# A planner-ordered attention and MLP kernel: the order planned with other durations, and batch 0's stores on another queue

## The chip, the cores and the metric

The kernel runs on one core of one Trainium2 chip. The metric is the time of the device in microseconds (us) from start to end of one execution.

## What is computed

A linear attention with positional weights is followed by a two-layer MLP with squared ReLU. Shapes: q, k, v are 8 batches x 8 heads x 576 positions x 64; the MLP maps 4608 tokens of width 512 to 2048 and back.

```python
theta = np.pi / 2.0 * pos / S            # pos = 0..575, S = 576
phi(x) = concatenate([relu(x) * cos(theta), relu(x) * sin(theta)])
kv  = einsum('bhsf,bhsd->bhfd', phi(k), v)
z   = sum(phi(k), axis=2)
num = einsum('bhsf,bhfd->bhsd', phi(q), kv)
den = einsum('bhsf,bhf->bhs', phi(q), z)[..., None] + 1e-06
x   = (num / den) as (tokens, 512)
out = relu(x @ w_in) ** 2 @ w_out        # float32
```

## The kernel before

**Tiles.** Each batch's 576 positions are four tiles of 128 tokens (J = 4) and a tail of 64. Per batch the work has these stages. A feature operation on ScalarE or VectorE makes relu(x) times the cosine or the sine for q and k (`declare_feature`, lines 406 and 408 in the profile), and a cast makes v bf16 (`declare_v`, line 413). TensorE forms kv and z per head (`declare_kz`; 65 columns, one being the sum), q is transposed, and the numerator and denominator follow (`declare_num`, which also divides on VectorE, lines 637 to 639). For batches 0 and 1 the transposing of q and x is done on TensorE (lines 591, 682), for batches 2 to 7 by DMA on the SyncE queue (`qpT`, `xT`, lines 575 and 667).

**The MLP.** Batches 0 to 2 multiply x by w1 plainly (`declare_plain`); batches 3 to 7 use seven products in place of eight (`declare_seven1`, with sums of x blocks from `declare_x_sums`). ReLU is on ScalarE (line 416), the square on VectorE (line 419), and VectorE's combined add and ReLU is line 422. The second layer is plain for batch 0 (`declare_rows`) and seven products for pairs of tiles after that (`declare_pair`, with sums of g blocks, `gs`, and of w2, `w2s`). All matmuls but the transposing ones are recorded at line 430, all VectorE sums at line 427. Tails of several batches go through the MLP together.

**Queues.** q, k and v of batch 0 are loaded from SyncE (SP) in a fixed prologue, w1 in four quarters from GpSimd (POOL). Loads of batches 1 and 2 and of w2 are on POOL, later ones on SP. Output is stored from a tile `ysb` (line 391): batch 0's two stores from POOL, the others from SP. The queue is chosen by `st_name` and `st_eng`.

**What sets the order.** The functions above only declare operations: an engine or a choice of engines with a duration in microseconds, the keys read and written, and for TensorE a place `pos`. A `Planner` then goes through a simulated time: at each step it takes the operation that can start earliest, by these durations, by free buffers and by a transfer's time, and among equals the one with the smallest slot (TensorE) or latest allowed time (`late`). The result is the order in which each engine gets its instructions. At run time each engine executes its list in order and waits on semaphores; the simulated times themselves have no effect. `SHIFTS` is a list of corrections: `81:-5.0` adds -5.0 us to the slot or `late` of operation number 81 in the order of declaration, and a third field (`:ACT`, `:DVE`) fixes its engine. The fourth argument of the planner is a margin added to the landing of every planned transfer:

```python
T_MM, T_MM128, T_MM65, T_TR = 0.1092, 0.0586, 0.0296, 0.066
plan = Planner(POOLS, 4.5, ("gs1", "gs2", "gs3", "gs4"), 1.0, SHIFTS)
...
o.done = pipe + (self.margin if e != "GIVEN" else 0.0)
```

In `declare_att(b, kpos, npos, cos_k, cos_q, cast)` the last three arguments are the engines allowed for the cosine features of k, those of q, and the casts of v; the defaults are either engine, VectorE and ScalarE.

Of the kernel before, what the change touches and what calls it, by code (L numbers as in the profile page):

```python
# [18 lines left out]


SHIFTS = """
23:9.5:ACT 37:-0.5 38:1.0 44:17.5:ACT 46:-1.0 53:-0.5 62:11.5 79:-2.0 85:-2.5 89:3.0 93:11.0
108:5.5 144:9.0 152:-2.0 157:9.5:ACT 191:-5.0 194:-1.0 202:-1.5 203:-3.5:ACT 204:2.0 210:3.0
238:2.5 241:2.5 243:5.0 249:-6.0 257:-4.0 260:-2.0 261:-6.0 270:2.5 271:3.5 287:-5.0 325:-2.0
335:-0.5 340:1.5 348:8.5 354:-7.0 364:-19.0 383:1.0 390:-3.5 392:1.0 417:-4.5 487:-5.0 492:1.5
516:-7.5 517:-5.5 530:39.0 533:25.5 546:9.0 563:5.5 565:12.5 573:-8.5 575:5.0 588:13.0 593:4.5
598:-2.0 611:-4.5 617:-5.5 636:-1.5 670:7.5 677:-2.0 690:1.0 698:0.0:DVE 702:22.5 703:-19.5
704:3.5:ACT 706:-4.0 715:2.0 731:-2.5 748:5.0 781:-4.5 783:-6.0 785:-7.0 787:-2.0 790:-1.0
794:-1.5 797:1.0 799:1.0 807:11.0 813:-5.5 817:-4.0 820:-7.0 822:-5.5 836:-3.5 850:-3.5
859:-34.0 860:-15.0 870:1.0 872:-4.0 884:12.0 890:49.0 893:17.0 906:5.5 907:23.5 911:3.0 917:3.0  # L30
936:-3.0 951:-12.5 957:-1.0 958:-1.5 963:-3.5 985:7.0 990:-4.0 998:3.5 1005:-4.5 1009:5.5
1023:-10.0 1024:-8.5 1030:-10.0 1041:-26.0:ACT 1042:-10.5 1133:-13.0 1143:1.5 1155:4.0 1157:3.0
1176:-4.5 1191:4.5 1209:5.5 1247:2.5 1306:-0.5
"""


# [197 lines left out]
def kernel(  # L234
# [9 lines left out]
    nc = tc.nc  # L244
# [7 lines left out]
    J = S // P  # L252
    MAIN = J * P
    TAIL = S - MAIN
    HH = H // 2
# [64 lines left out]
    def bank(buf):  # L320
        return banks[:, buf.i + (6 if buf.pool == "B" else 0), :]
# [104 lines left out]
    def sub(out, in0, in1, op=ALU.subtract):  # L426
        nc.vector.tensor_tensor(out=out, in0=in0, in1=in1, op=op)  # L427
# [102 lines left out]
    def declare_kz(b, pos, engs=("ACT",)):  # L530
        ba, bb = plan.buf("F"), plan.buf("F")
        kvz = kvzb[b] = plan.buf("kvz")
        for j in range(NS):

            def kz(_, j=j):
                kp, vx = at(kp_of(b, j)), at(vxb[b, j])
                for hh in range(HH):
                    for half in range(2):
                        h = half * HH + hh
                        if j < J:  # L540
                            lhsT, rhs = kp[:, h, :], vx[:, h, :]
                        else:
                            p0, p1 = half * TAIL, (half + 1) * TAIL
                            lhsT, rhs = kp[p0:p1, hh, :], vx[p0:p1, hh, :]
                        mm(
                            bank_pair(ba, bb)[:, half, hh * E1 : (hh + 1) * E1],
                            lhsT,
                            rhs,
                            j == 0 and hh == 0,
                            j == J and hh == HH - 1,  # L550
                        )

            add(
                ("PE", T_MM65 * (2 if j < J else 1) * HH + 0.02),
                kz,
                r=[(kp_of(b, j), j % 2, "c"), (kp_of(b, j), j % 2, "s"), vxb[b, j]],
                w=[ba, bb],
                pos=pos + 0.001 * j,
            )

        def kvz_copy(eng):
            dst = at(kvz).rearrange("p (a h) e -> p a (h e)", a=2)
            copy(eng, dst, bank_pair(ba, bb)[:, :, 0 : HH * E1])

        add({e: 0.5 if e == "ACT" else 0.6 for e in engs}, kvz_copy, r=[ba, bb], w=[kvz])
# [39 lines left out]
    def declare_num(b, j, pos):  # L605
        n = 2 if j < J else 1
        bks = [plan.buf("F") for _ in range(n)]
        pe = (b, "p", j) in qpTb
        qT = qpTb[b, "p", j] if pe else qpTb[b, j // 2]
        den = plan.buf("den")  # L610
        xbuf = x_of(b, j)

        def num(_):
            kvz, t = at(kvzb[b]), at(qT)
            h0 = 0 if pe or j == J else j % 2 * H
            for hh in range(HH):
                for half in range(2):
                    e0 = hh * E1
                    if j < J:
                        o = bank_pair(*bks)[:, half, e0 : e0 + E1]  # L620
                        lhsT = t[:, h0 + half * HH + hh, :]
                    else:
                        p0, p1 = half * TAIL, (half + 1) * TAIL
                        o = bank(bks[0])[p0:p1, e0 : e0 + E1]
                        lhsT = t[:, hh, p0:p1]
                    mm(o, lhsT, kvz[:, half * HH + hh, :], True, True)

        add(("PE", T_MM65 * n * HH + 0.015), num, r=[qT, kvzb[b]], w=bks, pos=pos)

        def div(_):  # L630
            if n == 2:
                n4 = bank_pair(*bks)
            else:
                n4 = banks[:, bks[0].i : bks[0].i + 1, :]
            n4 = n4[:, :, 0 : HH * E1].rearrange("p b (h e) -> p b h e", e=E1)
            d, r = at(den)[:, 0, 0:n], at(den)[:, 1, 0:n]
            nc.vector.tensor_single_scalar(out=d, in_=n4[:, :, :, D], scalar=EPS, op=ALU.add)  # L637
            nc.vector.reciprocal(out=r, in_=d)
            nc.vector.tensor_tensor(  # L639
                out=x_at(b, j).rearrange("p (b k) (l d) -> p b k l d", b=n, l=2),  # L640
                in0=n4[:, :, :, 0:D].rearrange("p b (k l) d -> p b k l d", l=2),
                in1=r.rearrange("p b (k l) -> p b k l", l=2)
                .unsqueeze(4)
                .to_broadcast([P, n, HH // 2, 2, D]),
                op=ALU.mult,
            )

        add(("DVE", 1.06 if j < J else 0.75), div, r=bks, w=[den, (xbuf, j % 2)])
# [147 lines left out]
    def declare_x_sums(b):  # L796
        buf = xsb[b] = plan.buf("xs")
        x0, x1 = xT_of(b, 0), xT_of(b, 1)
        a = lambda kk, half: at((x0, x1)[half])[:, kk * KB2 : (kk + 1) * KB2, :]
        t = lambda n: a(0, 1) if n == 3 else at(buf)[:, min(n, 3) - 1]  # L800
        xk = [[(x0, 0), (x0, 1)], [(x1, 0), (x1, 1)]]
        for n, ops, reads in (
            (1, lambda: (a(0, 1), a(0, 0)), xk[0] + xk[1]),
            (2, lambda: (a(1, 1), t(1)), xk[1] + [(buf, 1)]),
            (3, lambda: (a(1, 1), a(0, 1)), xk[1]),
            (4, lambda: (a(1, 0), t(2)), xk[0] + [(buf, 2)]),
        ):
            add(("DVE", 0.34), lambda _, n=n, ops=ops: sub(t(n), *ops()), r=reads, w=[(buf, n)] + (xk[1] if n == 3 else []))

    def declare_seven1(b, r, t):  # L810

# [11 lines left out]
        def product(name, off, acc, w, x, first, reads):  # L823
# [24 lines left out]
        product("P4", 13, Bk, lambda: w1_cols(1, 1, r), lambda: Tn(4), False, [key(1), (xs, 4)])  # L848
        add(("ACT", 0.5), lambda _: relu(block(1, 0), halves(bank(Bk))), r=[Bk], w=[(rows[1], 0)])
        add(  # L850
            ("DVE", 0.63), lambda _: add_relu(block(1, 1), halves(bank(E)), halves(at(u3))),
            r=[E, u3], w=[(rows[1], 1)],
        )
        product("P3", 14, E, lambda: w1_sum(4, r), lambda: X(1, 1), False, [("w1s", 4, r)] + xk[1])
        add(
            ("DVE", 0.63), lambda _: add_relu(block(0, 1), halves(bank(E)), halves(at(u2))),
            r=[E, u2], w=[(rows[0], 1)],
        )
        for i in range(2):
            hb = i * HBH + 2 * r  # L860
            if last:
                for j in range(2):
                    add(
                        ("DVE", 0.34),
                        lambda _, i=i, j=j, hb=hb: square(gT[:, hb : hb + 2, j * TP : (j + 1) * TP], block(i, j)),
                        r=[(rows[i], j), turn], w=[gkey(hb, j)],
                    )
            else:
                add(
                    ("DVE", 0.6), lambda _, i=i, hb=hb: square(gT[:, hb : hb + 2, :], at(rows[i])),  # L870
                    r=[(rows[i], 0), (rows[i], 1), turn], w=[gkey(hb, 0), gkey(hb, 1)],
                )
# [1 line left out]


    def st_name(b):
        return "SP" if b >= 1 else "POOL"

    def st_eng(b):
        return nc.sync if b >= 1 else nc.gpsimd  # L880

    def w2_block(i, j):
        return w2sb[:, i * HBH : (i + 1) * HBH, j * DM2 : (j + 1) * DM2]
# [38 lines left out]
    def declare_pair(b, pair, t):  # L922
# [7 lines left out]
        for n, ops, op, reads in (  # L930
# [2 lines left out]
            (3, lambda: (a(0, 0), a(1, 0)), ALU.subtract, gk(0)),  # L933
            (4, lambda: (a(0, 1), at(gs[2])), ALU.subtract, gk(1) + [gs[2]]),
        ):
            add(("DVE", 0.67 if n == 1 else 0.61), lambda _, n=n, ops=ops, op=op: sub(at(gs[n]), *ops(), op), r=reads, w=[gs[n]])
        acc = lambda x: bank(x)[:, 0:DM2]
        yb = lambda i, j: at(y)[:, i, j * DM2 : (j + 1) * DM2]
        u2, u3 = (lambda: at(u)[:, 0:DM2]), (lambda: at(u)[:, DM2:DM])
# [317 lines left out]
    declare_load(1, "v", "POOL", 23.0)  # L1257
    declare_w2_load(2, 25.0, 12.0)
    declare_w2_load(3, 26.0, 13.0)
    declare_att(1, T2[0] + 4.5, [T2[0] + x for x in (6.0, 9.0, 12.0, 14.0, 19.0)], BOTH, BOTH, BOTH)  # L1260
    for nm in "qkv":
        declare_load(2, nm, "POOL", 28.0)
    declare_rows(0, range(4), T2[0], 2)
    for s in range(8):
        for i in range(2):
            declare_plain(1, s % 4 * 4 + 2 * i, s // 4, T1[1] + s * 2 * PROD2 + i * PROD2, s == 0)
    declare_att(2, T2[1], [T2[1] + 1.7 + 1.75 * i for i in range(NS)], BOTH, BOTH, BOTH)
    for nm in "qkv":
        declare_load(3, nm, "SP", after=[turned["q", 2, J // 2]])
    declare_w2_sums()  # L1270
# [71 lines left out]
```

## Time and profile before

| | |
|---|---|
| three runs | 276.74, 278.27, 279.21 us (median 278.27) |
| profiled execution, its own time | 276.82 us |
| its span, first to last instruction | 274.8 us |
| TensorE matmul busy | 267.9 us (98%) |
| TensorE weight loads busy | 227.6 us (83%) |
| VectorE, ScalarE, GpSimd busy | 218.9, 194.9, 21.6 us |
| data moved | 53.01 MB, mean 193 GB/s |

The span is shorter than the execution's own time by 2.0 us. PE is TensorE's matmuls, PEld its weight loads, DVE VectorE, ACT ScalarE, POOL GpSimd, and SP SyncE, whose q stands for the queue's own instructions. A start time counts from the span's start. Matmuls overlap in the pipeline, so a group's length is more than the distance to the next group's start.

### The profile page before, as it was taken

How to read it: one execution, taken by the hardware profiler on the slowest of the kernel's cores; microseconds unless marked ns; L12 is line 12 of the kernel's file. 1: busy time of each engine (PE TensorE's matmuls, PEld its weight loads, DVE VectorE, ACT ScalarE, POOL GpSimd, SP SyncE). 2: the span in 40 equal slices, each digit the busy share in tenths (PEclk: the TensorE clock that was granted, in tenths of full speed). 3: DMA queues.
4: the chain of work that ended last, by engine and by line, in shares of the span. 5: the costliest groups of instructions: out<-in, count | busy, mean ns of one | idle time of the engine just before them, and what ended most of it. 6: DMA issues, size and time to landing. Idle time of an engine off the chain costs nothing.

```text
span 274.8 us, 7115 instructions
## 1 busy us (share of the span) xinstructions
PE 267.9 (98%) x2845; PEld 227.6 (83%) x2845; DVE 218.9 (80%) x515; ACT 194.9 (71%) x391; POOL 21.6 (8%) x38
## 2 busy tenths in 40 slices
PE   8979999999999999999999999999999999999994
PEld 3668856789988988888888898988988888888884
DVE  1789996997694989699968999799968798279652
ACT  3876982997895598589957994699735954684522
POOL 1453544010000000000000000000000000000000
PEclk9999999999999999999999999999999999999999
DMA  7999999969979998899299955996198301200025
GB/s 217 321 205 290 296 283 365 219 218 225 361 160 186 281 334 156 224 347 221 81 164 308 259 181 102 265 338 217 35 205 170 91 2 44 95 16 2 1 79 153
DMA packets 81840, 53.01 MB, mean 193 GB/s; under 512 B 53584, under 2 KB 77648, under 8 KB 81808
## 3 DMA queue, kind: packets, MB, share of 16 engines
q1 hardware_dynamic: 75136, 40.12, 58.4%
q0 software_dynamic: 6528, 12.32, 17.1%
q8 instruction: 22, 0.36, 0.5%
q10 hardware_dynamic: 144, 0.13, 0.1%
q14 instruction: 10, 0.08, 0.1%
HBM read 36.70 MB, written 9.44 MB: 168 GB/s over the span
## 4 chain that ended last, share of the span: by engine, by line
PE 80%; DMA 8%; DVE 7%; issue 1%; SPq 1%; POOL 1%; ACT 1%; DVEq 0%
PE banks L430 79%; DMA w1sb<-in_moe_w_in_dram 4%; DMA qpT<-qp 2%; DMA vt<-in_v_dram 2%; DVE rs L422 2%; DVE gT L419 2%; DVE gs L427 2%; PE banks L591 1%; DVE x L639 1%; POOL w1sb L373 1%; SPq L366 0%; PE banks L682 0%; DVE qp L408 0%; DVE kp L408 0%; SPq L358 0%
## 5 line engine op out<-in xcount | busy, mean ns | idle before, releaser
L430 PEld LDWEIGHTS <-w1sb 128*128 128x128 bf16 x784 | 73.0, 98 | 10.4 <-DMA w1sb<-in_moe_w_in_dram 1.4
L430 PE MATMUL banks<-xT,w1sb 128*128 128x256 bf16 (+1 forms) x576 | 68.4, 267 | 1.0 <-DMA w1sb<-in_moe_w_in_dram 1.0
L430 PEld LDWEIGHTS <-gs 128*128 128x128 bf16 x512 | 49.0, 98 | 5.9 <-DVE gs L427 0.2
L416 ACT ACTIVATE rt<-banks 128x512 bf16<-128x512 f32 x64 | 37.2, 600 | 14.9 <-PE banks L430 9.3
L430 PEld LDWEIGHTS <-gT 128*128 128x128 bf16 x400 | 38.0, 98 | 9.0
L430 PE MATMUL banks<-w2sb,gT 128*128 128x256 bf16 (+1 forms) x288 | 44.2, 296 | 0.0
L430 PEld LDWEIGHTS <-w1s 128*128 128x128 bf16 x320 | 30.7, 98 | 3.7
L430 PE MATMUL banks<-w2sb,gs 128*128 128x256 bf16 x256 | 33.0, 273 | 0.0
L430 PE MATMUL banks<-w2s,gs 128*128 128x256 bf16 x256 | 32.2, 273 | 0.0
L422 DVE CUSTOM_DVE_ANT_0 rs<-banks,sums 128x512 bf16<-128x512 f32 x40 | 27.0, 684 | 4.5 <-ACT sums L847 3.1
L419 DVE TENSOR_TENSOR gT<-rs 128x1024 bf16<-128x1024 bf16 (+1 forms) x50 | 27.7, 579 | 1.8 <-ACT rs L416 1.0
L416 ACT ACTIVATE rs<-banks 128x512 bf16<-128x512 f32 x40 | 23.6, 604 | 3.1 <-PE banks L430 2.9
L430 PE MATMUL banks<-xs,w1s 128*128 128x256 bf16 x160 | 23.0, 273 | 0.0
L430 PE MATMUL banks<-xT,w1s 128*128 128x256 bf16 x160 | 22.9, 273 | 0.0
L419 DVE TENSOR_TENSOR gT<-rt 128x512 bf16<-128x512 bf16 x48 | 19.2, 418 | 4.5 <-ACT rt L416 4.3
L427 DVE TENSOR_TENSOR ysb<-banks,sums 128x256 f32<-128x256 f32 x32 | 13.4, 418 | 11.2 <-PE banks L430 7.3
L406 ACT ACTIVATE qp<-q,sin_col 128x512 bf16<-128x512 f32 x31 | 22.1, 738 | 0.1
L639 DVE TENSOR_TENSOR x<-banks,den 128x512 bf16<-128x512 f32 x30 | 20.7, 691 | 1.0
L406 ACT ACTIVATE kp<-k,sin_col 128x512 bf16<-128x512 f32 x30 | 21.2, 734 | 0.0
L427 DVE TENSOR_TENSOR gs<-gT 128x1024 bf16<-128x1024 bf16 x28 | 19.2, 686 | 1.1 <-PE banks L430 0.7
L413 ACT CAST vx<-v 128x512 bf16<-128x512 f32 x26 | 16.2, 636 | 0.9 <-DMA v<-in_v_dram 0.9
L637 DVE TENSOR_SCALAR den<-banks 128x8 f32<-128x8 f32 (+1 forms) x38 | 6.0, 159 | 12.5 <-PE banks L430 12.3
(106 smaller groups left out, 364.0 us busy)
## 6 DMA issues: line engine op xcount, KB each, us to landing
out_dram<-ysb SPq DMA_DIRECT2D x13, 512.0 KB, 3.5
k<-in_k_dram SPq DMA_DIRECT2D x6, 1024.0 KB, 6.4
v<-in_v_dram SPq DMA_DIRECT2D x5, 1024.0 KB, 7.9
q<-in_q_dram SPq DMA_DIRECT2D x5, 1024.0 KB, 9.3
w1sb<-in_moe_w_in_dram POOLq DMA_DIRECT2D x4, 512.0 KB, 10.5
q<-in_q_dram POOLq DMA_DIRECT2D x2, 1024.0 KB, 11.2
w2sb<-in_moe_w_out_dram POOLq DMA_DIRECT2D x4, 512.0 KB, 11.6
k<-in_k_dram POOLq DMA_DIRECT2D x2, 1024.0 KB, 11.3
```

The lines of the kernel that those rows point to most:

```text
L373: nc.gpsimd.dma_start(out=w1sb[:, :, f0:f1], in_=moe_w_in[:, f0:f1].rearrange("(kb p) f -> p kb f", p=P),)
L406: nc.scalar.activation(out=dst, in_=src, func=ACTF.Relu, scale=col)
L413: (nc.scalar.copy if eng == "ACT" else nc.vector.tensor_copy)(out=out, in_=in_)
L416: nc.scalar.activation(out=out, in_=in_, func=ACTF.Relu)
L419: nc.vector.tensor_tensor(out=out, in0=in_, in1=in_, op=ALU.mult)
L422: nc.vector._custom_dve(TENSOR_ADD_SAT, out=out, in0=in0, in1=in1, s0=float("inf"), s1=0.0)
L427: nc.vector.tensor_tensor(out=out, in0=in0, in1=in1, op=op)
L430: nc.tensor.matmul(out=out, lhsT=lhsT, rhs=rhs, start=start, stop=stop, skip_group_check=True)
L591: nc.tensor.transpose(t[:, h, :], qp_at(b, j)[:, h, :], ident[:, :])
L637: nc.vector.tensor_single_scalar(out=d, in_=n4[:, :, :, D], scalar=EPS, op=ALU.add)
L639: nc.vector.tensor_tensor(out=x_at(b, j).rearrange("p (b k) (l d) -> p b k l d", b=n, l=2), in0=n4[:, :, :, 0:D].rearrange("p b (k l) d -> ...
```

## The change

It has four kinds of edits. The output stores of batch 0 go to the SP queue like all others. Durations given to the planner change: the tail groups of kv and numerator count eight small matmuls where they counted four, and several VectorE sums, squares and adds get 0.01 to 0.09 us more. For batches 1 and 2 the engines that may do the cosine features (and for batch 1 the casts) are restricted to VectorE. And `SHIFTS` is another list. Of the long list a few entries are shown.

```diff
 SHIFTS = """
-... 79:-2.0 85:-2.5 89:3.0 93:11.0 ... 690:1.0 ... 859:-34.0 860:-15.0 ... 1023:-10.0 1024:-8.5 1030:-10.0 ...
+... 81:-5.0 85:-8.5 89:7.0 91:1.0 92:3.5 97:2.5 102:2.0 ... 690:14.0 691:4.5 ...
+... 856:-5.0 857:-6.0 859:-9.0 ... 1024:-34.5 1026:-36.0 1030:-20.0 ...
 """
...
-                ("PE", T_MM65 * (2 if j < J else 1) * HH + 0.02),
+                ("PE", T_MM65 * (2 * HH) + 0.02),
...
-        add(("PE", T_MM65 * n * HH + 0.015), num, r=[qT, kvzb[b]], w=bks, pos=pos)
+        add(("PE", T_MM65 * 2 * HH + 0.015), num, r=[qT, kvzb[b]], w=bks, pos=pos)
...
-            add(("DVE", 0.34), lambda _, n=n, ops=ops: sub(t(n), *ops()), ...
+            add(("DVE", 0.43 if n == 3 else 0.36), lambda _, n=n, ops=ops: sub(t(n), *ops()), ...
...
-            ("DVE", 0.63), lambda _: add_relu(...        # twice in declare_seven1
+            ("DVE", 0.64), lambda _: add_relu(...
...
-                        ("DVE", 0.34),                   # the square of a batch's last round
+                        ("DVE", 0.37),
...
     def st_name(b):
-        return "SP" if b >= 1 else "POOL"
+        return "SP" if b >= 0 else "POOL"
     def st_eng(b):
-        return nc.sync if b >= 1 else nc.gpsimd
+        return nc.sync if b >= 0 else nc.gpsimd
...
-            add(("DVE", 0.67 if n == 1 else 0.61), ... w=[gs[n]])
+            add(("DVE", 0.72 if n == 1 else 0.62), ... w=[gs[n]])
...
-    declare_att(1, T2[0] + 4.5, [...], BOTH, BOTH, BOTH)
+    declare_att(1, T2[0] + 4.5, [...], DVE1, DVE1, DVE1)
...
-    declare_att(2, T2[1], [...], BOTH, BOTH, BOTH)
+    declare_att(2, T2[1], [...], DVE1, DVE1, BOTH)
```

The planner's call, with its margin, is not in the diff.

## The prediction

> **What bounds the kernel now.** I read four views in this order: the busy shares, the matmul timeline, the waits, and the busy time by stage. The first two lines are of the page.
>
> ```profile
> PE 267.9 (98%) x2845; PEld 227.6 (83%) x2845; DVE 218.9 (80%) x515; ACT 194.9 (71%) x391; POOL 21.6 (8%) x38
> ...
> PEclk9999999999999999999999999999999999999999
> ```
>
> TensorE is busy for 267.9 of 274.8 us at the full granted clock. That leaves 6.9 us of idle time, and 1.2 us of it lies ahead of the first matmul and 3.4 us behind the last, which ends at 271.3 us. A busy share hides small stalls, so I looked at distances between starts in the timeline of the matmuls. Its columns are start, length, engine, line, operation and count, and in brackets the idle time before.
>
> ```profile
> 17.72 1.06 PE L430 MATMUL banks<-xT,w1sb 128*128 128x128 bf16 x16
> 19.64 1.05 PE L430 MATMUL banks<-xT,w1sb 128*128 128x256 bf16 x8 [0.86 <-DMA w1sb<-in_moe_w_in_dram]
> 20.52 0.41 PE L430 MATMUL banks<-kvz,sums 128*128 128x65 bf16 x8
> 20.77 1.03 PE L430 MATMUL banks<-xT,w1sb 128*128 128x256 bf16 x8
> 21.64 0.39 PE L682 MATMUL banks<-ident,x 128*128 128x128 bf16 x4
> 22.19 1.05 PE L430 MATMUL banks<-xT,w1sb 128*128 128x256 bf16 x8 [0.16 <-DMA w1sb<-in_moe_w_in_dram]
> ...
> 122.35 1.04 PE L430 MATMUL banks<-xTt,w1sb 128*128 128x256 bf16 x8
> 123.73 0.60 PE L430 MATMUL banks<-xs,w1sb 128*128 128x256 bf16 x4 [0.34 <-ACT sums L847]
> ...
> 142.47 0.60 PE L430 MATMUL banks<-xT,w1sb 128*128 128x256 bf16 x4
> 143.26 0.42 PE L430 MATMUL banks<-kvz,qpT 128*128 128x65 bf16 x8 [0.20 <-DMA qpT<-qp]
> ```
>
> Eight matmuls of 256 columns start 0.87 us before the next group (20.77 to 21.64), so one takes 0.109 us; one of 128 columns takes 0.056 us (23.07 to 23.29 for four), one of 65 takes 0.030 us. From these the stalls follow. 17.72 plus 16 x 0.057 is 18.63, and the next group starts at 19.64: 1.01 us, for the second quarter of w1. 21.64 plus 0.22 is 21.86, then 22.19: 0.33 us, for the third quarter. 122.35 plus 0.87 is 123.22, then 123.73: 0.51 us. 142.47 plus 0.44 is 142.91, then 143.26: 0.35 us. The same sum on the group of 97.97 us gives 0.18 us. Together these five make 2.38 us. Between 13.2 and 16.5 us, where batch 0's attention is a chain through all engines, another 1.0 us is lost. So **3.4 us is all that a better order can win**; the rest is matmul work, start and end.
>
> The tail of each batch (64 tokens) shows a third thing.
>
> ```profile
> 40.53 1.14 PE L430 MATMUL banks<-vx,kp 128*128 128x65 bf16 x32
> 41.59 0.30 PE L430 MATMUL banks<-vxt,kpt 64*128 64x65 bf16 x8
> 41.83 1.04 PE L430 MATMUL banks<-w2sb,gT 128*128 128x512 bf16 x4
> ```
>
> 40.53 plus 32 x 0.0296 is 41.48; the next full-size group begins at 41.83. The eight tail matmuls cost 0.35 us, where the planner counts 4 x 0.0296 + 0.02 = 0.14 us.
>
> **What the Trainium skill says.** "Trainium Kernel Development and Optimization", Performance Expectations, calls matmul busy time a bad metric because matmuls are pipelined; this trace agrees, since 98% busy holds the stalls just worked out. "TensorEngine Tiling (Array Packing)", Key Properties, says that changing the tiling mode drains TensorE; that fits the 0.35 us, about 0.1 us on each side of the eight small matmuls. "DMA: Bandwidth & Descriptors", Issuing engines are not separate DMA queues, says that the SP and POOL queues run on the same engines and that another issuer saves issue time alone. The page of before gives 3.5 us (SP) and 4.9 us (POOL) from issue to landing of a 512 KB store, at different loads.
>
> **Part 1: batch 0's stores from POOL to SP.** Two transfers of 512 KB change their queue.
>
> ```profile
> 52.37 0.61 POOL L391 DMA_DIRECT2D out_dram<-ysb  x1 [6.07 <-ACT ysb L1020]
> 55.54 0.69 POOL L391 DMA_DIRECT2D out_dram<-ysb  x1 [2.55 <-ACT ysb L1020]
> ...
> 51.14 11.44 SPq L575 DMA_TRANSPOSE qpT<-qp  x2
> ```
>
> They are POOL's last two instructions, so its 8.6 us of waiting held up nobody and is worth nothing when it goes. SP gets two issues of about 0.4 us (its stores later show 0.38 and 0.53), into a gap: the line of 51.14 us is two transposes of batch 2, the second issued at 60.18 us. Queued behind them there are that second transpose, the tail's at 62.68 us, and batch 3's loads from 64.01 us. The first transpose of batch 2 lands by 58.2 us (51.14 plus at most 7.0, the longest landing of qpT) and its first reader starts at 71.8 us. A store that waits for its copy up to 55.5 us leaves that slack standing. Cost: 0; if the cover is gone, as much as the store is late beyond some 7 us.
>
> **Part 2: batches 1 and 2, cosine features and casts on VectorE alone.** In the ScalarE timeline six of these ran on ScalarE: two of q (28.58 and 48.67 us), one of k (38.13), one k tail (46.27) and two casts of batch 1 (39.25). Batch 2's casts stay free. On VectorE the same forms follow each other at 0.39 us (k, four in 1.66 us), 0.26 us (tail) and 0.34 us (cast): 3 x 0.39 + 0.26 + 2 x 0.34 = 2.1 us added. ScalarE loses 3 x 0.61 + 0.41 + 2 x 0.53 = 3.3 us.
>
> ```profile
> 24.00:34.00 10.00, 10.00 (x97) 8.59 (x95) 9.86 (x29) 8.26 (x16) 4.41 (x6) 1.00 1.12 303
> 34.00:50.00 16.00, 16.00 (x162) 9.51 (x161) 13.05 (x30) 10.18 (x20) 6.45 (x9) 1.00 1.11 321
> 50.00:62.00 12.00, 12.00 (x139) 10.14 (x136) 11.60 (x34) 11.88 (x23) 1.30 (x2) 1.00 0.86 205
> ```
>
> The third number is TensorE, then weight loads, VectorE and ScalarE. VectorE has 38 - 34.5 = 3.5 us free from 24 to 62 us, so 2.1 us fit, and the sums of w1 and w2 in that stretch have no early reader and can give way. TensorE has no stall there now. Result on the end: 0, with +1 us if a square or a feature is made late.
>
> **Part 3: corrected durations.** No instruction changes; only the planner's clock does. Fifteen tail groups (kv of batches 1 to 7 and the numerators of all eight) get 0.12 us more each, 1.8 us in all. Without it the plan lets TensorE be too early by 0.2 us a tail, 15 x 0.21 = 3.1 us at the end. Small sums on VectorE get 0.01 to 0.09 us more; the trace shows 686 ns for the first gs sum where the plan had 0.67 and now has 0.72. The effect cannot be read off a row. Below it is bounded by the three steady stalls (1.04 us gone), above by tighter packing: a TensorE that was slower than planned gave every other engine up to 3 us of unplanned slack, and this is now cut to about 1.3 us.
>
> **Part 4: the order.** Nearly all shifts differ. Counting declared operations gives their names. Three of batch 0 matter: 81 (transposing x for tile 3) has -5.0 and 85 (transposing the q tail) goes from -2.5 to -8.5, while the first w1 products 91, 92 and 102 get +1.0, +3.5 and +2.0. So eight transposing matmuls, now at 23.07 and 23.29 us and behind the w1 waits, are drawn ahead of them: 8 x 0.056 = 0.45 us of the 1.34 us filled. The w1 loads themselves do not move (issued from 9.1 us, in the fixed prologue). Bounds: 0 to 1.34 us; I take 0.5. For the three later stalls I take 1.04 gone and 0.5 come up elsewhere, since any order leaves a few places that the durations miss. The order of loads on SP in batches 5 to 7 also changes much (690, 856, 857, 859, 1024, 1026); counted at 0 and kept as a rival.
>
> **Part 5: the care of one microsecond.** The diff has no line of it: the Planner call of before already carries 1.0 as its margin. Worth 0.
>
> **Sum.** 0.5 + 1.04 - 0.5 = 1.0 us gained. The profiled execution took 276.82 us (span 274.8 and 2.0 around it), so 275.8 us. Of the runs before that one is at the low end (276.74 to 279.21, median 278.27), so I carry the gain to the median: **277.3 us**. About 1%, 2.8 us, is what a measurement of this kernel can tell from no change.
>
> **Rivals.**
> *The order empties the whole pool.* The w1 wait, batch 0's chain and the later stalls nearly all go, and runs that are slower than the profiled one lose their longer transfer waits as well. For it: the median is 1.45 us above the profiled run, and waits on transfers are what can vary. Against it: w1 lands when it lands. 278.27 - 3.2 = 275.1 us.
> *The stalls only change places.* Every plan with TensorE packed meets two or three misjudged waits. 278.3 us.
> *Slower: a transposed tile behind one more load.* SP issues in order and loads of 1 MB pass at 366 GB/s at the peak of the page, 2.9 us each. The wait at 143.26 us shows a qpT with no slack left at batch 5. If a load of batch 5, 6 or 7 now stands ahead of a q transpose there, TensorE's numerator waits 2.9 us more, and the slack that the old clock gave is gone. It decides once the load is ahead of the transpose by less than its 2.9 us. For it: those loads have the largest shifts. Against it: the planner counts the shared transfer engines. 278.27 + 2.9 = 281.2 us.
> *That the change does not do what it says* is true of part 5 alone.
>
> **How the numbers follow.** Forecast 0.44, whole pool 0.26, same 0.14, slower 0.16. Faster by over 1% is the whole pool and a tenth of the forecast, 0.30; slower by over 1% is the last less a little, 0.14; the rest, 0.56, lies within. The range runs from 275.0 (pool) to 279.8 us (half of the slower case left out).
>
> **What would show it.** Right: the two w1 waits, 1.34 us now, near 0.9 us together; the groups at 123 and 143 us at their even distance; both stores on SP near 52 to 56 us; VectorE above 11.6 of 12 us near 50 to 62 us without a TensorE stall. Wrong: a TensorE gap above 1 us behind 24 us, most of all before a numerator on qpT.

## The result, and the profile after

The changed kernel takes **281.36 us** (median, 280.21 to 282.72); the kernel before took 277.52 us (four runs, 276.74 to 279.21). The ratio is 1.0129, with a 95% interval of 1.0089 to 1.0169: **slower by 1.3%**. A ratio here is estimated from the single runs of both kernels, so it isn't quite the quotient of the two medians. The forecast was 277.3 us, with a range from 275.0 to 279.8 us. Wrong, in direction too.

The profiled execution of after took 282.72 us (span 280.6). It is the slowest of its four runs, and that of before (276.82 us) is near its fastest, so the two profiles lie 5.9 us apart where the medians lie 3.8 us apart. The head of its page looks almost as it did:

```profile
PE 270.5 (96%) x2841; PEld 227.3 (81%) x2846; DVE 221.7 (79%) x522; ACT 191.0 (68%) x384; POOL 22.1 (8%) x36
...
PEclk9999999999999999999999999999999999999999
```

TensorE's share falls from 98 to 96% at an unchanged clock. ScalarE is 3.9 us less busy and VectorE 2.8 us more, which is about part 2 as it was worked out. Neither is near its limit over the whole span. The matmul timeline shows more: the columns are as before, and only lines with one of the larger stalls or beside one are copied.

```profile
17.82 1.95 PE L431 MATMUL banks<-xT,w1sb 128*128 128x128 bf16 x32
20.30 1.05 PE L431 MATMUL banks<-xT,w1sb 128*128 128x256 bf16 x8 [0.54 <-DMA w1sb<-in_moe_w_in_dram]
21.19 0.41 PE L431 MATMUL banks<-kvz,sums 128*128 128x65 bf16 x8
...
95.14 3.65 PE L431 MATMUL banks<-xT,w1sb 128*128 128x256 bf16 x32 [0.71 <-ACT rt L417]
...
120.87 0.60 PE L431 MATMUL banks<-xs,w1s 128*128 128x256 bf16 x4
122.43 0.60 PE L431 MATMUL banks<-xT,w1s 128*128 128x256 bf16 x4 [0.95 <-ACT sums L845]
123.41 0.60 PE L431 MATMUL banks<-xs,w1s 128*128 128x256 bf16 x4 [0.39 <-ACT banks L841]
...
160.51 0.60 PE L431 MATMUL banks<-xT,w1s 128*128 128x256 bf16 x4 [0.58 <-DVE rs L423]
...
177.50 1.04 PE L431 MATMUL banks<-w2sb,gs 128*128 128x256 bf16 x8
179.12 0.60 PE L431 MATMUL banks<-xT,w1s 128*128 128x256 bf16 x4 [0.59 <-ACT sums L845]
...
183.21 0.60 PE L431 MATMUL banks<-xT,w1s 128*128 128x256 bf16 x4
184.19 0.42 PE L431 MATMUL banks<-kvz,qpT 128*128 128x65 bf16 x8 [0.38 <-DMA qpT<-qp]
```

By distances between starts: 120.87 plus 4 x 0.109 is 121.31, and the next group starts at 122.43, so 1.12 us are lost; then 0.54 us ahead of 123.41; 0.75 us ahead of 179.12; 0.54 us ahead of 184.19. The same sum gives 0.87 us ahead of 95.14 and 0.75 us ahead of 160.51. Not copied are 0.42 us ahead of 114.78 us (released by VectorE's division, `den`) and three gaps of 0.2 to 0.3 us behind 92 us. TensorE writes its products to the banks of PSUM (`banks`), and ScalarE or VectorE must read a bank out before the program's next product can go there. The releasers of all copied gaps but two are such reads: a relu (`rt`), copies (`sums`, `banks`) and VectorE's add and ReLU (`rs`); there TensorE waits for a bank. The two others are the DMA of w1 at 20.30 us and a transpose (`qpT`) at 184.19 us.

Why are these reads late? The ScalarE timeline of after at the largest gap:

```profile
118.15 0.57 ACT L841 COPY banks<-banks 128x512 f32<-128x512 f32 x1
120.69 0.72 ACT L407 ACTIVATE kp<-k,sin_col 128x512 bf16<-128x512 f32 x1 [1.97 <-DMA k<-in_k_dram]
121.32 0.58 ACT L417 ACTIVATE rs<-banks 128x512 bf16<-128x512 f32 x1
121.80 0.58 ACT L845 COPY sums<-banks 128x512 f32<-128x512 f32 x1
122.26 0.61 ACT L417 ACTIVATE rs<-banks 128x512 bf16<-128x512 f32 x1
122.75 0.61 ACT L841 COPY banks<-banks 128x512 f32<-128x512 f32 x1
```

and the same stretch of before:

```profile
117.07 0.60 ACT L416 ACTIVATE rs<-banks 128x512 bf16<-128x512 f32 x1 [0.59 <-PE banks L430]
117.56 0.58 ACT L844 COPY sums<-banks 128x512 f32<-128x512 f32 x1
118.03 0.61 ACT L416 ACTIVATE rs<-banks 128x512 bf16<-128x512 f32 x1
118.52 0.61 ACT L840 COPY banks<-banks 128x512 f32<-128x512 f32 x1
119.03 0.73 ACT L406 ACTIVATE kp<-k,cos_col 128x512 bf16<-128x512 f32 x1
```

They are the same four operations. In before, the first feature of batch 5's k stands behind them and its load had landed at 118.33 us. In after it stands ahead of them, at a load that landed at 120.67 us. ScalarE waits 1.97 us there, the four reads are held behind it, and TensorE runs out of banks. The feature itself is in no hurry: the first matmul that reads batch 5's features starts at 133.68 us, more than 10 us later. The Trainium skill says ("PSUM — Partial Sum Buffer", Engine vs sequencer instructions) that the queues of ScalarE and VectorE are strict FIFO; this trace agrees, since the four reads behind the feature start only from 121.32 us on, one after the other and with no wait of their own.

The waits of ScalarE on loads, from 24 us on, as the waits view of after has them (total us, times, longest):

```profile
ACT kp L407 <- DMA k<-in_k_dram: 4.4, 4, 2.0
...
ACT qp L407 <- DMA q<-in_q_dram: 0.7, 2, 0.4
ACT kpt L407 <- DMA kt<-in_k_dram: 0.6, 1, 0.6
```

Before had 0.5 us on k and 0.9 us on v. A table by stage shows where the time went. Each entry is the distance between starts less the matmuls' own lengths (0.216, 0.109, 0.056, 0.030 us by columns; 0.039 us for one of a tail's eight), summed over the stage, in us. The first column also holds some 7 us of matmuls that only fill the time before the first data. What follows the last matmul start (3.6 to 4.0 us) is left out. A few matmul records can be missing from a trace (2841 in after, 2846 in the fullest), which adds some tenths to the first two columns.

| kernel | median us | ratio | to 30 us | 30-92 | 92-132 | 132-192 | 192-end |
|---|---|---|---|---|---|---|---|
| before | 277.52 | 1 | 13.99 | 0.34 | 1.04 | 0.67 | 0.16 |
| after | 281.36 | 1.0129 | 14.61 | 0.84 | 3.80 | 2.98 | 0.19 |

By this sum the two profiled executions differ by 6.2 us, and 5.1 us of it lie between 92 and 192 us. The 0.6 us up to 30 us can't be told from the scatter of start-up: see the last section.

### The profile page after: what moved, and what is told of

The parts are those of the page before. It is cut to its first block, busy times and chain, and to the rows that moved or that the text cites. A ratio compares the mean times of both kernels' runs of the same rounds, so it can differ in the third digit from the quotient of the medians.

```text
span 280.6 us, 7125 instructions
## 1 busy us (share of the span) xinstructions
PE 270.5 (96%) x2841; PEld 227.3 (81%) x2846; DVE 221.7 (79%) x522; ACT 191.0 (68%) x384; POOL 22.1 (8%) x36
## 4 chain that ended last, share of the span: by engine, by line
PE 67%; DMA 13%; DVE 5%; ACT 3%; SPq 2%; issue 2%; DVEq 0%; ACTq 0%
PE banks L431 66%; DMA k<-in_k_dram 6%; DMA q<-in_q_dram 4%; DMA qpT<-qp 3%; DVE gT L420 1%; SPq L367 1%; DVE rs L423 1%; PE banks L592 1%; DVE gs L428 1%; SPq L576 1%; ACT rt L417 1%; ACT kp L407 0%; DVE x L640 0%; PE banks L683 0%; ACT rs L417 0%
## 5 line engine op out<-in xcount | busy, mean ns | idle before, releaser
L420 DVE TENSOR_TENSOR gT<-rs 128x1024 bf16<-128x1024 bf16 (+1 forms) x50 | 28.3, 582 | 4.4 <-ACT rs L417 3.6
L431 PE MATMUL banks<-xs,w1s 128*128 128x256 bf16 x160 | 23.7, 273 | 0.4 <-ACT banks L841 0.4
L407 ACT ACTIVATE kp<-k,sin_col 128x512 bf16<-128x512 f32 x29 | 20.2, 723 | 4.4 <-DMA k<-in_k_dram 4.4
L431 PE MATMUL banks<-xTt,w1sb 128*128 128x256 bf16 x128 | 16.3, 273 | 0.0
```

The costliest lines, as they stand in the source:

```text
L407: nc.scalar.activation(out=dst, in_=src, func=ACTF.Relu, scale=col)
L420: nc.vector.tensor_tensor(out=out, in0=in_, in1=in_, op=ALU.mult)
L431: nc.tensor.matmul(out=out, lhsT=lhsT, rhs=rhs, start=start, stop=stop, skip_group_check=True)
```

## The experiments

Each ratio below is against runs of before made beside that kernel's own, whose medians went from 277.15 to 278.19 us.

Theory: **head-of-line waiting**. The new order puts features and casts where their loads are planned to land; the loads land later, and the reads queued behind them cost TensorE its banks. Rivals: the whole order is so tight that any move costs (places trade against each other); the stores on SP; the 2.1 us more on VectorE; start-up. Where two numbers of operations are paired below, the first is moved to stand right behind the second in the planner's finished order, and no other operation changes its place:

```diff
+def moved(order, behind):
+    order = list(order)
+    by_n = {o.n: o for o in order}
+    for n, ref in behind:
+        order.remove(by_n[n])
+        order.insert(order.index(by_n[ref]) + 1, by_n[n])
...
-        for op in plan.plan(t0):
+        for op in moved(plan.plan(t0), MOVES):
```

### All features by their loads, later or sooner

Three kernels move those features and casts of batches 3 to 7 that are planned within 4 us of their load's landing and at least 5 us ahead of their first reader (57 operations in after, 47 in before), by a fixed distance in the planner's time:

```diff
+            if landed is not None and op.eng in ("ACT", "DVE") and op.start >= 60 and op.start - landed < 4.0:
+                if min(x.start for x in op.succ) > op.end + 5.0:
+                    by[op] = 4.0          # after_later, before_later; -2.0 in after_sooner
...
-        for op in plan.plan(t0):
+        for op in rearranged(order, by):
```

After, 4 us later:

> The changed kernel with its own plan, but 57 features and casts of k, v and q of batches 3 to 7, which the plan puts within 4 us of the landing of their load, stand 4 us later in the order of ScalarE and VectorE. TensorE's, SP's and POOL's orders are the same. Theory A (in-order ScalarE and VectorE stand at a feature whose load has not landed, and the reads of PSUM behind it keep TensorE): the TensorE gaps at 94, 121 to 123, 160 and 178 us shrink or go, about 3 us of the 4.8 us lost after 90 us come back, near 278 us. Rival B (a q transpose behind loads on SP, as in the prediction): nothing of this changes, 281 us. Rival C (the tighter plan leaves too little room on ScalarE and VectorE, whatever the loads do): no gain, perhaps a loss, 281 to 283 us.

Measured: 286.33 us, ratio 1.0319 (1.0273 to 1.0365). The waits of ScalarE on loads of q, k and v are all gone, and so are the gaps at 95 and 122 us. But others take their places, as features now crowd the reads of other stretches. As idle time in brackets, which is some 0.16 us less than by starts: 0.40 us ahead of 101.10 us (`rt`), 0.47 us ahead of 105.85 us (`ysb`), and most of all 0.93 and 0.78 us ahead of 152.95 and 164.31 us (both `sums`).

After, 2 us sooner:

> The same 57 features and casts of the changed kernel 2 us sooner in the order of ScalarE and VectorE than the plan has them. Theory A: each batch's first wait on a load grows by up to 2 us and more of it reaches TensorE: 2 to 5 us slower than the changed kernel, 283 to 286 us. Rivals B and C: within 1 us of the changed kernel.

Measured: 288.39 us, ratio 1.0389 (1.0348 to 1.0430). ScalarE's wait on k grows to 6.9 us and on the k tail to 2.4 us, and TensorE idles 1.17 us ahead of 94.90, 1.77 us ahead of 121.19 and 1.20 us ahead of 126.04 us.

Before, 4 us later:

> The kernel before with 47 features and casts, chosen by the same rule, 4 us later on ScalarE and VectorE. Theory A: its waits on loads there sum to 3 us from 24 us on and hardly reach TensorE, so 0 to 0.5 us faster, 277 us. Rival C: the moved work crowds a later stretch, 0.5 to 2 us slower.

Measured: 283.98 us, ratio 1.0230 (1.0188 to 1.0271), again with gaps from crowding (0.59 us ahead of 104.66 us, `rt`).

What follows: each of the three is slower than any case that was written down for it. A bulk move costs 1.9 and 2.6% more in the kernel after, later and sooner, and 2.3% in the kernel before, so these three can't separate the theory from the rival of a tight order. They show that both mechanisms exist.

### Seven features put back

```diff
+MOVES = [(523, 439), (525, 488), (534, 451), (693, 644), (883, 824), (885, 883), (1030, 956)]
```

> The kernel after, with seven feature instructions (the first k features of batches 4, 5 and 7 on ScalarE, two k features of batch 4, two q features of batch 6 on VectorE), which stood at a load that had not landed, each put one to four places further back on its engine, behind the PSUM reads that were ready and queued behind it. Everything else in the order stays. Head-of-line theory: the TensorE gaps at 94, 121 to 123, 160 and 179 us (0.87, 1.67, 0.75 and 0.75 us by distance of starts, 4.0 us) go, and with them 3 to 4 us: 277.5 to 278.5 us, level with before within 0.5%. Rival (the finely packed plan gives every gain back at the next place, as the bulk moves seemed to show): 280 us or more. Rival (the loss sits in start-up and the stores, not in these places): no change, 281.4 us.

Measured: 279.93 us, ratio 1.0077 (1.0054 to 1.0100). The gaps at 95, 122, 160 and 179 us are gone or small, and one has come up. The matmul timeline and the ScalarE timeline of this kernel (its lines are numbered 14 higher):

```profile
125.12 0.60 PE L445 MATMUL banks<-xT,w1s 128*128 128x256 bf16 x4 [1.64 <-ACT sums L859]
```

```profile
123.60 0.51 ACT L421 ACTIVATE kpt<-kt,sin_col 128x256 bf16<-128x256 f32 x1 [1.77 <-DMA kt<-in_k_dram]
124.02 0.58 ACT L431 ACTIVATE rs<-banks 128x512 bf16<-128x512 f32 x1
124.49 0.58 ACT L859 COPY sums<-banks 128x512 f32<-128x512 f32 x1
```

The wait moved to the next load in the queue: the k tail of batch 5, whose feature had been covered by the wait ahead of it. The expectation of 277.5 to 278.5 us was missed for that reason.

### Fourteen features put back

```diff
+MOVES = [(523, 439), (526, 433), (528, 436), (525, 488), (534, 451), (693, 644), (699, 635),
+         (705, 637), (695, 624), (704, 640), (883, 824), (885, 883), (1030, 956), (1029, 945)]
```

> The kernel after with fourteen features put one to four places back behind PSUM reads (the seven of the run before this, and those of the same loads that stood in front next: k features 526, 528, 699 and the k tail 705 on ScalarE, 695, 704 and 1029 on VectorE). SP and TensorE keep their orders. Head-of-line theory: the 1.64 us gap at 125 us that the seven moves left behind (ScalarE at the k tail of batch 5) goes too, so 277.7 to 278.7 us, ratio 0.999 to 1.004. Rival (what is won in one place is lost in the next): no better than with seven moves, ratio 1.008 or more.

Measured: 279.60 us, ratio 1.0072 (1.0045 to 1.0099). This lies between the two cases expected, and it can't be told from the seven moves (1.0077). In the profile ScalarE has no wait on a load of k or v left behind 80 us, and of TensorE's gaps from 92 to 132 us 3.80 us have become 1.71. Two are left there that have another cause, one of them this:

```profile
99.90 0.32 PE L445 MATMUL banks<-kvz,qpTt 128*64 128x65 bf16 x8 [0.78 <-ACT rt L431]
```

Here ScalarE waits for no load. It is late with `rt` after a wait of 1.07 us for a square of VectorE, at 95.44 us, and five features and casts of batch 4 that are done among the reads of 93.6 to 98.8 us. The largest gap behind 132 us has a third cause, a transposed tile:

```profile
180.78 0.42 PE L445 MATMUL banks<-kvz,qpT 128*128 128x65 bf16 x8 [0.60 <-DMA qpT<-qp]
```

So the theory holds for its gaps, but not for the whole loss: from 1.0129 to 1.0072 less than half came back, and the two intervals still overlap.

### The mirror in the kernel before

```diff
+MOVES = [(522, 433), (692, 628), (883, 734), (885, 883), (1030, 961)]
```

> The mirror: the kernel before, with the first k feature of batches 4, 5 and 7 on ScalarE and the first two q features of batch 6 on VectorE put one to five places ahead, so that each stands at its load before this has landed and holds back PSUM reads as in the kernel after (waits of about 1.5, 1.9, 1.4 and 1.4 us). Nothing else changes, SP's and TensorE's orders included. Head-of-line theory: TensorE gaps of 0.5 to 1.2 us come up at about 95, 118, 151 and 179 us, together 3 to 4 us, so 281 to 282 us (ratio 1.011 to 1.015). Rival (banks and slack absorb single waits, and after is slow for other reasons): within 0.3% of before, 277.5 to 278.5 us.

Measured: 281.44 us, ratio 1.0109 (1.0036 to 1.0182). The time is as expected, though the interval is wide. The ScalarE timeline and the matmul timeline of this kernel:

```profile
118.12 0.72 ACT L420 ACTIVATE kp<-k,cos_col 128x512 bf16<-128x512 f32 x1 [1.72 <-DMA k<-in_k_dram]
118.74 0.58 ACT L430 ACTIVATE rs<-banks 128x512 bf16<-128x512 f32 x1
119.22 0.57 ACT L858 COPY sums<-banks 128x512 f32<-128x512 f32 x1
```

```profile
119.85 0.60 PE L444 MATMUL banks<-xT,w1s 128*128 128x256 bf16 x4 [1.15 <-ACT sums L858]
...
155.55 0.60 PE L444 MATMUL banks<-xs,w1s 128*128 128x256 bf16 x4 [0.86 <-ACT banks L854]
```

Five operations on two engines, and no other change, make of the kernel before one that is as slow as after, with releasers of the same kind; a third gap lies ahead of 182.46 us (1.35 us by starts). From 92 to 192 us the profile loses 5.2 us where before lost 1.7. The move at batch 4 gave a wait of 0.83 us and no gap, so not every such wait reaches TensorE.

### Stores and cosine features alone

Stores alone, in the kernel before (the two lines of `st_name` and `st_eng`; the order stays the same otherwise):

> The kernel before with the one part that batch 0's two stores are issued from SP. By the planner no other instruction changes its place. The prediction's part 1: 0 us, 277.5 us. Rival: SP's later list is shifted by the two issues and the drift of the SP queue begins here, 1 us or more slower.

Measured: 278.72 us, ratio 1.0035 (1.0004 to 1.0066). Cosine features and casts alone:

```diff
+        order = plan.plan(t0)
+        for op in order:
+            if op.n in (153, 157, 162, 172, 318, 327):
+                op.eng = "DVE"
```

> Part 2 alone: the kernel before, with its own order, and the four cosine features (q twice, k, k tail) and two casts of batches 1 and 2 that ScalarE had given to VectorE at the same places of the order. The prediction's 0: within 0.3% of before. Rival (2.1 us more of VectorE at 24 to 62 us delays squares or sums there): 0.5 to 1.5 us slower with a TensorE gap at 40 to 62 us.

Measured: 278.76 us, ratio 1.0048 (1.0028 to 1.0068). Both together, in the order of before:

> Parts 1 and 2 alone: the order of the kernel before, unchanged, with batch 0's stores on SP and the six instructions on VectorE. If the two small losses (0.35 and 0.48%) add: ratio 1.006 to 1.010. If they are one and the same small delay: 1.003 to 1.005. By the prediction: within 0.3% of before.

Measured: 278.41 us, ratio **1.0005** (0.9984 to 1.0025). Each alone seemed to cost something and both together cost nothing, so a difference under 0.5% isn't to be read as an effect in this kernel, even where its interval leaves out 1. The runs of before beside the second and the third of these had medians of 277.26 and 277.97 us, which is 0.26% apart with no change at all. The other half, the new order with stores on POOL and the six instructions on ScalarE:

> Parts 3 and 4 alone: the order of the kernel after, unchanged, with batch 0's stores issued by POOL and the four cosine features and two casts on ScalarE, as in the kernel before. If the order carries the loss: ratio 1.010 to 1.015 (280 to 281.5 us). If stores and features carry most of it: 1.002 to 1.007.

Measured: 280.07 us, ratio **1.0079** (1.0051 to 1.0108). This lies between the two cases expected; with 1.0005 for the other half, the larger part of the loss goes with the order. Its ScalarE and matmul timelines show the same picture at the same batch:

```profile
124.03 0.51 ACT L407 ACTIVATE kpt<-kt,sin_col 128x256 bf16<-128x256 f32 x1 [1.40 <-DMA kt<-in_k_dram]
```

```profile
125.55 0.60 PE L431 MATMUL banks<-xT,w1s 128*128 128x256 bf16 x4 [1.20 <-ACT sums L845]
```

In this execution the gaps at 160 and 179 us are missing; batch 6's q landed 1.3 us earlier than in after (157.57 us) and batch 7's k 2.9 us earlier (174.72 us).

### The lateness of the loads

In after the first store of batch 1 stands on SP behind the loads of batch 4, and transposes of batch 3 behind it; before had issued it at 78.13 us. `MOVES = [(385, 478)]` puts it early again:

> The kernel after, with one store alone moved: the first store of batch 1 is issued on SyncE at about 79.5 us, behind the first q transpose of batch 2, as before had it at 78.1 us, and not behind batch 4's loads at 97.9 us. ScalarE, VectorE and TensorE keep their orders. Theory that batch 5's loads are late because the store stood in SP's queue ahead of x transposes of batch 3 and what follows: k of batch 5 lands 1 to 2 us earlier than 120.7 us, the ScalarE wait on it shrinks from 1.97 to under 1 us, and the time falls by 0.5 to 1.5 us (280 to 280.9 us). Rival (loads are late because TensorE itself is, so the q transposes ahead of them are): landing within 0.7 us of 120.7, time unchanged at 281.4 us.

Measured: 281.66 us, ratio 1.0143 (1.0043 to 1.0244). The load of batch 5's k landed at 118.29 us (2.4 us earlier) and ScalarE's wait at it fell from 1.97 to 0.77 us, as expected; but the waits at batch 4's k (1.68 us, 1.05 in after) and batch 6's q (1.20 us on VectorE, 0.95 in after) were longer, and the time didn't fall. With the seven moves as well:

> Both moves together: the seven features behind the ready PSUM reads and the batch 1 store early. If the two causes act apart: about 277 to 278 us; if both act through the same wait: no more than the features alone.

Measured: 281.54 us, ratio 1.0121 (1.0041 to 1.0202); with the fourteen:

> The same fourteen moves, and batch 1's first store issued early on SyncE (about 79.5 us). If lateness of loads no longer matters once nothing stands behind them, the same as the fourteen moves alone within 0.3%; if the lateness still costs, 0.5 to 1 us less.

Measured: 279.93 us, ratio 1.0085 (1.0054 to 1.0115), the same as the fourteen alone within the noise. No gain from an earlier store shows.

### Where the rest is

Three kernels went on from the fourteen moves. Four more moves on ScalarE, `(528, 445), (524, 448), (1033, 968), (1036, 961)`:

> The kernel with fourteen features put back, and four more moves on ScalarE: a k feature and a v cast of batch 4 and two k features of batch 7 each one to three places back, behind PSUM reads that TensorE waited for at 98.8 us (0.94) and 179.9 us (0.76). Theory that the order of ScalarE against these reads is the rest of the loss: those two gaps go, 1.0 to 1.7 us faster than with fourteen moves, ratio 1.001 to 1.004. Rival (the rest lies in stores and cosine features): ratio unchanged at 1.006 to 1.008.

Measured: 279.86 us, ratio 1.0100 (1.0068 to 1.0132). The gap at 99 us fell from 0.94 to 0.38 us, but 0.19 and 0.50 us came up at 101 and 104 us: here the rival of a tight order fits, since in a stretch that is full a gain at one place came back at the next. The gap at 180 us stayed (0.79). Two of the four moves were meant for it, but no read on ScalarE releases it: TensorE waits for the second q transpose of batch 6. In the kernel with fourteen moves, as in after, SP issues this transpose behind the loads of batch 7:

```profile
167.43 1.10 SPq L373 DMA_DIRECT2D k<-in_k_dram  x1
168.58 0.64 SPq L373 DMA_DIRECT2D v<-in_v_dram  x1
...
171.97 5.28 SPq L590 DMA_TRANSPOSE qpT<-qp  x1
```

In before it stood ahead of them:

```profile
170.27 2.03 SPq L575 DMA_TRANSPOSE qpT<-qp  x1
172.34 0.93 SPq L358 DMA_DIRECT2D k<-in_k_dram  x1
```

It landed 4.88 us after its issue in before, 8.90 us in after and 8.76 us with fourteen moves. No kernel here moved this transpose alone.

The fourteen moves with the stores on POOL:

> The kernel with fourteen features put back, and batch 0's two stores issued by POOL again, the order of every other queue unchanged. If the stores on SP carry part of the rest, as in the kernel before alone (+0.35%): 0.5 to 1.5 us faster, ratio 1.002 to 1.006. By the prediction's part 1 (0): ratio 1.007.

Measured: 279.39 us, ratio 1.0084 (1.0054 to 1.0113). With the six instructions on ScalarE:

> The kernel with fourteen features put back, and the four cosine features and two casts of batches 1 and 2 on ScalarE again, at the places of the order where VectorE has them. If VectorE's 2.1 us more carry part of the rest, as alone (+0.48%): 0.5 to 1.8 us faster, ratio 1.001 to 1.005. If this order has room for them on VectorE (the plan was made with them there) and none on ScalarE: ratio 1.007 or more.

Measured: 279.35 us, ratio 1.0080 (1.0057 to 1.0103). And the eighteen moves with both undone:

> All together: eighteen moves, stores on POOL, the six instructions on ScalarE. If the parts add: level with the kernel before or better, 275.5 to 277.5 us, ratio 0.994 to 1.001. If they do not: above 1.004.

Measured: 280.65 us, ratio 1.0102 (1.0063 to 1.0140). None won anything, and the parts don't add: the plan was made with the six on VectorE.

The kernel before has a small wait of the same kind (0.86 us at a v load, 0.51 us of TensorE ahead of 123.73 us). `MOVES = [(522, 439), (703, 660)]` takes it away:

> The kernel before, with the first k feature of batch 4 one place back and the last v cast of batch 5 four places back on ScalarE, behind PSUM reads that are ready. Head-of-line theory: before's own stalls at 98.7 us (0.19) and 123.1 us (0.51) go: 0.5 to 0.7 us faster, ratio 0.997 to 0.999; the rival, that single waits are absorbed: no change.

Measured: 277.06 us, ratio 0.9997 (0.9978 to 1.0016). The gap at 123 us is gone from the profile; a gain of 0.5 us, which is 0.2%, can't be told from none. No version here beats the kernel before.

| kernel | ratio | to 30 us | 30-92 | 92-132 | 132-192 | 192-end |
|---|---|---|---|---|---|---|
| before, features ahead | 1.0109 | 14.07 | 0.34 | 1.85 | 3.36 | 0.17 |
| before, stores and cosines | 1.0005 | 14.99 | 1.23 | 0.85 | 0.98 | 0.10 |
| after, order alone | 1.0079 | 14.59 | 1.01 | 3.31 | 0.62 | 0.21 |
| after, seven back | 1.0077 | 14.56 | 0.35 | 3.35 | 1.03 | 0.16 |
| after, fourteen back | 1.0072 | 14.97 | 0.54 | 1.71 | 1.43 | 0.19 |
| after, eighteen back | 1.0100 | 14.49 | 0.54 | 1.97 | 1.60 | 0.19 |
| after, all 4 us later | 1.0319 | 14.36 | 1.52 | 2.60 | 5.21 | 0.67 |
| after, all 2 us sooner | 1.0389 | 13.84 | 2.27 | 5.57 | 5.90 | 0.29 |

Each row is one profiled execution beside a ratio from several runs, so a row is good to about a microsecond.

## Why the prediction was wrong

**The step that failed is the last term of part 4**: "For the three later stalls I take 1.04 gone and 0.5 come up elsewhere, since any order leaves a few places that the durations miss." The first half was near: the stalls of 98.7 and 143 us are gone. The second was mis-sized by a factor of about ten: in the profiled execution 6.8 us are lost from 92 to 192 us, where before lost 1.7. The 0.5 was taken from no row. The view that could have sized it was at hand: in before, ScalarE waits 0.86 us at a v load, and the one stall of TensorE behind it (0.51 us) is released by a copy queued behind that cast. The prediction read this stall by its releaser, "ACT sums", and asked when TensorE would be free of it; it did not ask what the copy had stood behind. Read that way, one cast ahead of its load costs 0.5 us.

The number of such places would not have sized the loss, since the plan of after has 57 (the ones that were moved in bulk) and that of before 47. Their distances might have. The plans that the two kernel files compute put the first k feature of batches 4, 5, 6 and 7 at 0.06, 1.18, 1.07 and 1.44 us behind the planned landing in before, and at 0.00, 0.03, 0.00 and 0.24 us in after. The margin of one microsecond is inside these landings, but batch 5's k landed 4.7 us later than planned in after (120.67 against 116.00 us), while the read ahead of its feature ran 2.6 us later than planned (118.15 against 115.53 us). That left the feature about 2 us ahead of its load.

**Part 4, loads.** "The order of loads on SP in batches 5 to 7 also changes much …; counted at 0 and kept as a rival." Counted at 0, it was wrong too. The rival named a q transpose behind a load, in front of TensorE's numerator, at 2.9 us. That gap came: batch 6's second transpose stands behind batch 7's loads, and TensorE loses 0.54 us ahead of 184.19 us, and 0.76 us in the kernel with fourteen moves. So the rival was right in kind, at a fifth to a quarter of its size; in the other profiles of the new order the gap there is anything from none to 1.00 us. Most of the loss came from the landings of k and q in front of features. The slower case's 281.2 us is close to the measured 281.4, by another mechanism: the number was luck. The sign that the prediction named for being wrong, a TensorE gap above 1 us, came at 122 us, but before a product on w1s.

**Part 4, the first w1 products.** 0.5 of 1.34 us, said the prediction. In after the second quarter's wait is 0.69 us (17.82 plus 32 x 0.056 is 19.61, then 20.30) and the third's is 0, so 0.65 us were won there, although the second quarter landed 0.66 us later in this execution (20.25 us, 19.59 before). As far as one profile of each shows, it was right, and hidden by the rest of start-up.

**Part 1, stores at 0**: right. SP issued them in the gap, with the second transpose of batch 2 behind them as before:

```profile
50.73 5.12 SPq L576 DMA_TRANSPOSE qpT<-qp  x1
55.95 0.99 SPq L392 DMA_DIRECT2D out_dram<-ysb  x2
60.03 3.05 SPq L576 DMA_TRANSPOSE qpT<-qp  x1
```

**Part 2, VectorE at 0**: right. Parts 1 and 2 together give 1.0005. The busy time by stage, TensorE third and VectorE fifth:

```profile
34.00:50.00 16.00, 15.84 (x147) 9.22 (x148) 13.37 (x35) 7.91 (x15) 7.70 (x9) 1.00 1.10 292
50.00:62.00 12.00, 11.95 (x143) 9.95 (x142) 11.76 (x33) 10.26 (x20) 0.42 (x1) 1.00 1.00 250
```

VectorE is busy 11.76 of 12 us and TensorE has 0.05 us idle, as the prediction's last paragraph asked.

**Part 3** was named with the right fear ("tighter packing: a TensorE that was slower than planned gave every other engine up to 3 us of unplanned slack") and then left out of the sum. Whether it was the corrected durations or the new corrections that put the features at the loads was not tried: the two belong to one plan, and the list of shifts can't be used with other durations without giving a third order. **Part 5** is 0: not in the diff.

**The sum** was 1.0 us gained; measured are 3.6 us lost (0.0129 x 277.5). The order alone gives 2.2 us of it (0.0079 x 278). What makes up the difference between 1.0079 and 1.0129 stays open; the intervals overlap, and undoing stores or features on top of the fourteen moves won nothing. Open too is the 0.7% that the fourteen moves left. In its profile 1.7 us show as two gaps: 0.95 us ahead of 99.90 us, where ScalarE is full, and 0.76 us ahead of 180.78 us, at the transpose behind the loads. Four more moves on ScalarE bought nothing, and what the transpose costs by itself is not shown.

## What to carry to other kernels

When an engine that empties PSUM also does work on loaded data, look for each first use of a load in its queue: what stands behind that instruction, and how much later may it be put? A use with 10 us to spare belongs behind the reads that TensorE needs, not at the planned landing. Read a stall's releaser one step further back, to what the releaser itself was queued behind, and price a new order by how close behind its planned landing each first use stands. Moves in bulk show little here, since they crowd the reads elsewhere; five chosen moves in the good kernel that bring about a loss of the same size say more than the repairs in the bad one, which brought back less than half.

## What was unexpected of the hardware

Up to 30 us nearly nothing differs between these kernels in what is loaded, and still the time lost there ranges from 13.73 to 14.99 us in eighteen of the profiled executions and is 15.61 and 17.49 us in two others, with no relation to the kernel. In the one of before the first quarter of w1 landed at 16.34 us, in the one of after at 17.68 us. The profiled execution of before was at the low end by that measure.

Later loads scatter too: with SP's order unchanged, batch 5's k took 6.60 us from issue to landing in after, 7.00 with seven moves, 6.17 with fourteen and 5.36 with all features 4 us later. With 1.6 us between the shortest and the longest, a plan that puts a feature within a microsecond of such a landing can be right in one execution and wrong in another.

A small load queued behind large ones landed after them: in after a k tail was issued at 115.37 us, behind the k and v loads of 1 MB, and landed at 124.02 us, 0.2 us after the v load. With seven moves the two loads of the k tail landed at 123.35 and 123.52 us, again right behind the v load (123.13 us), and so the tail's feature came to wait 1.77 us once the k feature ahead of it no longer did.
